# Chunked attention and a maxout layer on one core: where the attention weights of the stacked tiles are transposed

## The chip, the core and the metric

One core of one Trainium2 chip runs the whole program. The metric is the device time of one execution in microseconds; lower is better. Kernels are compared by the median of their runs.

## What is computed

Attention within chunks of 64 positions (8 batches, 8 heads, 576 positions, head size 64), then three products, their maximum, and a last product. All of it is float32:

```
scores = (1 / 8) * q_c @ k_c.T        # q_c, k_c, v_c: chunks of 64 x 64
attn   = exp(scores - max); attn = attn / (sum + 1e-9)
x      = (attn @ v_c), heads side by side      # 4608 tokens x 512
h      = max(x @ w1, x @ w2, x @ w3)           # 4608 x 768
out    = h @ w_out                             # 4608 x 512
```

## The kernel before, in words

The 4608 tokens are 36 tiles of 128 tokens (two chunks, eight heads), and nine groups of four tiles. A group's layer (`moe`) is 18 times 12 products (`hidden`, `pm` in PSUM) and 72 products of the projection (`project`); each product is three matmuls of fp32r (lines 145 to 147), since a float32 value is carried as a high and a low part.

While TensorE works on the layer of group i - 1, the attention of group i is put between its matmuls. TensorE's order is written out by hand: `due` (line 442) gives every step of every tile a time in a count of matmul time, and the loop at the end emits the attention's steps as their times come up. The other engines and the DMA queue (SP) have no order of their own in the source: a scheduler sets it from the data and from the buffers.

Ten tiles are plain. The other 26 are "stacked" (`attention`, line 249), and the change is about these. Their six steps, with their due times in units of that count, are `operands` (-8), `scores(0)` (0), `scores(1)` (2.9), `transpose` (16.5), `values(0)` (25.0) and `values(1)` (28.2). The next tile's `scores(0)` comes 16.3 after this tile's, so tile t's transpose stands right behind `scores(0)` of tile t + 1. Below, t is the tile whose weights are transposed.

- `operands` loads q and k (`r`, 1 MB) and v (`rv`, 512 KB), both with their rows twice, and makes `qs` and `kk`: ScalarE rounds to fp32r, GpSimd subtracts for the low part (`stack`, `split`).
- `scores(c)` runs four matmuls of 256 columns for chunk c into `s` (PSUM, one buffer); ScalarE copies and VectorE adds the two halves into `e`. After c = 1 comes the softmax (VectorE, GpSimd, ScalarE, and at its end GpSimd's multiplication at line 162), and `vs` is made of `rv` (ScalarE line 256, GpSimd line 257).
- `transpose` turns `e` by four TensorE transposes into `tp`; ScalarE and VectorE split it into high and low parts in half of the rows of `aa`, and two DMAs copy each half to the other rows:

```
tp = ps_t.tile([P, 4, P], F32, name="tp")
for g in range(4):
    nc.tensor.transpose(out=tp[:, g, :], in_=..., identity=ident)
...
for c, rows in enumerate(halves_of):
    nc.sync.dma_start(out=aa[halves_of[1 - c], c].bitcast(F32), in_=aa[rows, c].bitcast(F32))
```

- `values(c)` multiplies `vs` by `aa` for chunk c into `x`; `xs` collects the sums, and `xh`, `xl` are the layer's input.

Buffers matter: `aa`, `rv`, `qs`, `kk` and `xs` have one each, `vs` has two (by t modulo 2), `e` has two.

Of the kernel before, what the change touches and what calls it, by code (L numbers as in the profile page):

```python
# [8 lines left out]
F32 = mybir.dt.float32  # L9
F32R = mybir.dt.float32r  # L10
# [4 lines left out]
ALU = mybir.AluOpType  # L15
# [3 lines left out]
B, H, S, D = 8, 8, 576, 64  # L19
P = 128  # L20
# [5 lines left out]
PLAIN = 10  # L26
# [25 lines left out]
def chunk_attn_maxout_kernel(  # L52
# [12 lines left out]
    nc = tc.nc  # L65
# [2 lines left out]

    att = ctx.enter_context(tc.tile_pool(name="att", bufs=1))
    xs_p = ctx.enter_context(tc.tile_pool(name="xs_p", bufs=1))  # L70
    ep = ctx.enter_context(tc.tile_pool(name="ep", bufs=2))
    xp = ctx.enter_context(tc.tile_pool(name="xp", bufs=2))
    hpool = ctx.enter_context(tc.tile_pool(name="hpool", bufs=JT))
    tmp = ctx.enter_context(tc.tile_pool(name="tmp", bufs=2))
# [2 lines left out]
    ps_s = ctx.enter_context(tc.tile_pool(name="ps_s", bufs=1, space=PSUM))  # L77
    ps_t = ctx.enter_context(tc.tile_pool(name="ps_t", bufs=1, space=PSUM))
    ps_x = ctx.enter_context(tc.tile_pool(name="ps_x", bufs=1, space=PSUM))
    ps_m = ctx.enter_context(tc.tile_pool(name="ps_m", bufs=3, space=PSUM))  # L80

    ident = cpool.tile([P, P], F32, name="ident")
# [7 lines left out]
    def split(hi, lo, src, eng=nc.vector):  # L90
        nc.scalar.copy(out=hi, in_=src)  # L91
        eng.tensor_tensor(out=lo, in0=src, in1=hi.bitcast(F32), op=ALU.subtract)  # L92
# [84 lines left out]
    def plain_steps(t, x_of, col):  # L177


        st = {}  # L180

        def load_qk():
            st["r"] = att.tile([P, 1536], F32, name="buf", tag=("raw", "kk", "aa")[t % 3], bufs=1)
            nc.sync.dma_start(out=st["r"], in_=qk[t])

        def load_v():
            st["v"] = att.tile([P, 4, 2, P], F32, name="buf", tag=f"vs{t % 2}", bufs=1)
            nc.sync.dma_start(out=st["v"], in_=vb[t].rearrange("p (g c x) -> p g c x", g=4, c=2))

        def scores():  # L190
            r = st["r"]
            st["s"] = s = ps_s.tile([P, 8, 64], F32, name="s")
            for h in range(8):
                nc.tensor.matmul(out=s[:, h, :], lhsT=r[:, h * P:(h + 1) * P],  # L194
                                 rhs=r[:, 1024 + h * 64:1024 + (h + 1) * 64], start=True, stop=True)

        def maximum():
            st["mx"] = tmp.tile([P, 8], F32, name="mx")
            nc.vector.tensor_reduce(out=st["mx"], in_=st["s"], axis=AX.X, op=ALU.max)

        def less():
            st["e"] = ep.tile([P, 8, 64], F32, name="e")
            nc.vector.tensor_tensor(out=st["e"], in0=st["s"],
                                    in1=st["mx"].unsqueeze(2).broadcast_to([P, 8, 64]), op=ALU.subtract)

        def exp():
            nc.scalar.activation(out=st["e"], in_=st["e"], func=AF.Exp, scale=SCALE)

        def total():
            total, st["guard"], st["invert"], st["norm"] = over_sum(st["e"])  # L210
            total()

        def transpose():
            st["tp"] = tp = ps_t.tile([P, 4, P], F32, name="tp")
            for g in range(4):
                nc.tensor.transpose(out=tp[:, g, :], in_=st["e"][:, 2 * g:2 * g + 2].rearrange("p h k -> p (h k)"),  # L216
                                    identity=ident)

        def transposed():
            st["at"] = xs_p.tile([P, 4, P], F32, name="xs")  # L220
            nc.scalar.copy(out=st["at"], in_=st["tp"])

        def values():
            st["x"] = x = ps_x.tile([P, 4, P], F32, name="x")
            for g in range(4):
                for c in range(2):
                    nc.tensor.matmul(out=x[:, g, c * 64:(c + 1) * 64], lhsT=st["v"][:, g, c, :],  # L227
                                     rhs=st["at"][:, g, c * 64:(c + 1) * 64], start=True, stop=True)

        def high():  # L230
            nc.scalar.copy(out=x_of()[0][:, :, col:col + P], in_=st["x"])

        def low():
            xh, xl = x_of()
            nc.vector.tensor_tensor(out=xl[:, :, col:col + P], in0=st["x"],
                                    in1=xh[:, :, col:col + P].bitcast(F32), op=ALU.subtract)

        return dict(q=load_qk, v=load_v, S=scores, mx=maximum, sub=less, exp=exp, sum=total,
                    eps=lambda: st["guard"](), rec=lambda: st["invert"](), nrm=lambda *eng: st["norm"](*eng),
                    T=transpose, at=transposed, V=values, xh=high, xl=low)  # L240
# [6 lines left out]
    halves_of = [slice(0, 64), slice(64, 128)]  # L247

    def attention(t, x_of, col):

        st = {}

        def stack(hi, src):
            nc.scalar.copy(out=hi, in_=src)  # L256
            nc.gpsimd.tensor_tensor(out=hi[64:], in0=src[64:], in1=hi[64:].bitcast(F32), op=ALU.subtract)  # L257

        def products(pool, name, c, lhs, rhs, out):
            o = pool.tile([P, 4, 2, 2, 64], F32, name=name)  # L260
            for g in range(4):
                nc.tensor.matmul(out=o[:, g].rearrange("p a h x -> p (a h x)"), lhsT=lhs[:, c, g, :],  # L262
                                 rhs=rhs[:, c, g].rearrange("p a x -> p (a x)"), start=True, stop=True)
            for h, rows in enumerate(halves_of):
                nc.scalar.copy(out=out[rows], in_=o[rows, :, 0, h, :])  # L265
            for h, rows in enumerate(halves_of):
                nc.vector.tensor_tensor(out=out[rows], in0=o[rows, :, 1, h, :], in1=out[rows], op=ALU.add)  # L267

        def operands():
            r = att.tile([P, 2, 2, 4, P], F32, name="r", tag="raw", bufs=1)  # L270
            nc.sync.dma_start(out=r, in_=qk2[t - PLAIN])
            rv = att.tile([P, 2, 4, P], F32, name="rv", tag="rv", bufs=1)
            nc.sync.dma_start(out=rv, in_=v2[t - PLAIN])
            qs = att.tile([P, 2, 4, P], F32R, name="qs", tag="qs", bufs=1)
            stack(qs, r[:, 0])
            kk = att.tile([P, 2, 4, 2, P], F32R, name="kk", tag="kk", bufs=1)
            for c in range(2):
                split(kk[:, c, :, 0, :], kk[:, c, :, 1, :], r[:, 1, c], nc.gpsimd)
            st.update(rv=rv, qs=qs, kk=kk)

        def scores(c):
            if c == 0:
                st["e"] = ep.tile([P, 4, 2, 64], F32, name="e")
            products(ps_s, "s", c, st["qs"], st["kk"], st["e"][:, :, c, :])
            if c == 1:
                ef = st["e"].rearrange("p g c k -> p (g c) k")
                softmax(ef)
                vs = st["vs"] = att.tile([P, 2, 4, P], F32R, name="vs", tag=f"vs{t % 2}", bufs=1)
                stack(vs, st["rv"])

        def transpose():
            tp = ps_t.tile([P, 4, P], F32, name="tp")
            for g in range(4):
                nc.tensor.transpose(out=tp[:, g, :], in_=st["e"][:, g].rearrange("p c k -> p (c k)"), identity=ident)  # L294
            st["aa"] = aa = att.tile([P, 2, 4, 2, P], F32R, name="aa", tag="aa", bufs=1)
            for c, rows in enumerate(halves_of):
                nc.scalar.copy(out=aa[rows, c, :, 0, :], in_=tp[rows])
            for c, rows in enumerate(halves_of):
                nc.vector.tensor_tensor(out=aa[rows, c, :, 1, :], in0=tp[rows],
                                        in1=aa[rows, c, :, 0, :].bitcast(F32), op=ALU.subtract)  # L300
            for c, rows in enumerate(halves_of):
                nc.sync.dma_start(out=aa[halves_of[1 - c], c].bitcast(F32), in_=aa[rows, c].bitcast(F32))

        def values(c):
            if c == 0:
                st["xs"] = xs_p.tile([P, 4, P], F32, name="xs")
            products(ps_x, "x", c, st["vs"], st["aa"], st["xs"][:, :, c * 64:(c + 1) * 64])
            if c == 1:
                xh, xl = x_of()
                split(xh[:, :, col:col + P], xl[:, :, col:col + P], st["xs"], nc.gpsimd)  # L310

        return [operands, lambda: scores(0), lambda: scores(1), transpose, lambda: values(0), lambda: values(1)]

    outputs = []
# [138 lines left out]
    with tc.manual_schedule(engines={mybir.EngineType.PE}):  # L453
        for i in range(1, len(GROUPS)):
            g = moe(starts[i], lambda i=i: x_tiles(i))
# [49 lines left out]
```

## Time and profile before

| | |
|---|---|
| median of 3 runs | 713.27 us (713.2 to 714.03) |
| the profiled execution | 713.1 us, span 711.4 us |
| TensorE clock | 2.4 GHz over the whole span (granted clock 1.0) |
| busy share | PE 99%, DVE 56%, ACT 51%, POOL 43% |
| DMA | 90.28 MB moved, 38.5% of the 16 engines' time |

The span is the time from the first to the last instruction in the trace; the execution's own time lies 1.7 us above it. Busy PE is not PE at its peak: matmuls overlap in the pipeline, so the time that one adds is read from the distance between two starts, not from its duration.

### The profile page before, as it was taken

The page shows a single profiled execution, that of the slowest core. Times are in us where ns is not written, and L with a number is a line of the kernel's source. Part 1 is how long each engine was busy: PE and PEld are TensorE (multiplying, and loading weights), DVE is VectorE, ACT ScalarE, POOL GpSimd, SP SyncE. Part 2 cuts the span into 40 slices and gives each one's busy share as a digit, 9 for nine tenths or more (in the row PEclk, how much of TensorE's full clock was granted, in tenths as well). Part 3 has the DMA queues.
Part 4 walks back from the last instruction along what each step waited for, and adds up shares of the span by engine and source line. Part 5 has one row for each costly group of instructions (what it writes and reads, how often), then busy time and mean ns, then how long its engine had stood idle before and what let it go on. Part 6 is the DMA issues. An engine that isn't in the chain of part 4 may idle for free.

```text
span 711.4 us, 9743 instructions
## 1 busy us (share of the span) xinstructions
PE 703.1 (99%) x3545; PEld 592.9 (83%) x3546; DVE 398.9 (56%) x677; ACT 359.8 (51%) x665; POOL 308.9 (43%) x207
## 2 busy tenths in 40 slices
PE   8999999999999999999999999999999999999997
PEld 5997888888888888888888888888888888888886
DVE  7989852456456655676466637664566456521220
ACT  6675551445555555555555555556555655331111
POOL 2443020245656665555665555555566656100000
PEclk9999999999999999999999999999999999999999
DMA  9975640233433354333523363335333541120001
GB/s 365 410 275 185 195 139 31 88 117 114 149 124 119 111 144 131 119 118 84 184 90 118 119 177 119 119 120 171 120 105 107 160 134 33 30 75 15 1 1 59
DMA packets 23215, 90.28 MB, mean 127 GB/s; under 512 B 2944, under 2 KB 2944, under 8 KB 19840
## 3 DMA queue, kind: packets, MB, share of 16 engines
q1 hardware_dynamic: 23168, 89.67, 38.5%
q8 instruction: 28, 0.46, 0.3%
q14 instruction: 19, 0.16, 0.1%
HBM read 66.58 MB, written 9.44 MB: 107 GB/s over the span
## 4 chain that ended last, share of the span: by engine, by line
PE 95%; DMA 2%; DVE 1%; issue 1%; ACT 1%; SPq 0%; POOL 0%; ACTq 0%; DVEq 0%
PE pm L145 27%; PE pm L146 27%; PE pm L147 27%; PE s L262 3%; PE x L262 3%; PE x L227 2%; PE s L194 2%; PE tp L294 2%; DMA buf<-in_w 1%; DMA buf<-in_wout 1%; PE tp L216 1%; ACT ao L117 0%; SPq L108 0%; ACT kk L91 0%; POOL e L162 0%
## 5 line engine op out<-in xcount | busy, mean ns | idle before, releaser
L145 PE MATMUL pm<-xh,wl 128*128 128x512 f32 (+1 forms) x660 | 258.9, 392 | 0.3 <-ACT m L336 0.3
L146 PE MATMUL pm<-xl,wh 128*128 128x512 f32 (+1 forms) x660 | 255.3, 387 | 0.0
L147 PE MATMUL pm<-xh,wh 128*128 128x512 f32 (+1 forms) x660 | 254.9, 386 | 0.0
L147 PEld LDWEIGHTS pm<-xh,wh 128*128 128x128 f32 x660 | 124.1, 188 | 25.8
L145 PEld LDWEIGHTS pm<-xh,wl 128*128 128x128 f32 x660 | 124.4, 188 | 22.7 <-ACT m L336 0.7
L146 PEld LDWEIGHTS pm<-xl,wh 128*128 128x128 f32 x660 | 124.5, 189 | 21.7
L338 DVE TENSOR_TENSOR m<-pm,m 128x512 f32<-128x512 f32 (+1 forms) x110 | 74.9, 681 | 116.1 <-PE pm L147 95.2
L257 POOL TENSOR_TENSOR qs<-r,qs 64x1024 fp32r<-64x1024 f32 x26 | 62.5, 2402 | 148.2 <-ACT qs L256 148.1
L257 POOL TENSOR_TENSOR vs<-rv,vs 64x1024 fp32r<-64x1024 f32 x26 | 62.3, 2397 | 62.5 <-ACT vs L256 62.5
L347 DVE TENSOR_TENSOR hl<-m,hh 128x512 fp32r<-128x512 f32 (+1 forms) x54 | 75.3, 1394 | 17.7 <-ACT hh L344 17.3
L145 PE MATMUL pm<-woh,hl 128*128 128x512 f32 x216 | 85.0, 394 | 0.0
L265 ACT COPY e<-s 64x256 f32<-64x256 f32 x104 | 38.1, 366 | 91.9 <-PE s L262 91.3
L146 PE MATMUL pm<-wol,hh 128*128 128x512 f32 x216 | 84.4, 391 | 0.0
L147 PE MATMUL pm<-woh,hh 128*128 128x512 f32 x216 | 84.2, 390 | 0.0
L267 DVE TENSOR_TENSOR e<-s,e 64x256 f32<-64x256 f32 x104 | 43.8, 421 | 63.6 <-ACT e L265 62.9
L344 ACT CAST hh<-m 128x512 fp32r<-128x512 f32 (+1 forms) x55 | 33.5, 610 | 85.9 <-DVE m L338 85.9
L92 POOL TENSOR_TENSOR kk<-r,kk 128x512 fp32r<-128x512 f32 x52 | 66.7, 1297 | 6.2 <-ACT kk L91 5.7
L267 DVE TENSOR_TENSOR xs<-x,xs 64x256 f32<-64x256 f32 x104 | 43.8, 421 | 30.5 <-ACT xs L265 28.0
L265 ACT COPY xs<-x 64x256 f32<-64x256 f32 x104 | 38.0, 365 | 31.7 <-PE x L262 30.3
L162 POOL TENSOR_TENSOR e<-e,sm 128x512 f32<-128x512 f32 x31 | 32.3, 1043 | 47.0 <-DVE sm L159 43.9
L336 ACT COPY m<-pm 128x512 f32<-128x512 f32 (+1 forms) x55 | 31.8, 579 | 35.6 <-DVE hl L347 22.0
L147 PEld LDWEIGHTS pm<-woh,hh 128*128 128x128 f32 x216 | 40.6, 188 | 8.7
(67 smaller groups left out, 831.4 us busy)
## 6 DMA issues: line engine op xcount, KB each, us to landing
r<-in_qk SPq DMA_DIRECT2D x26, 1024.0 KB, 4.9
rv<-in_v SPq DMA_DIRECT2D x26, 512.0 KB, 3.3
aa<-aa SPq DMA_DIRECT2D x52, 256.0 KB, 3.3
out_x<-ao SPq DMA_DIRECT2D x36, 256.0 KB, 3.6
buf<-in_qk SPq DMA_DIRECT2D x10, 768.0 KB, 7.8
buf<-in_w SPq DMA_DIRECT2D x10, 512.0 KB, 4.5
buf<-in_vb SPq DMA_DIRECT2D x10, 512.0 KB, 6.7
buf<-in_wout SPq DMA_DIRECT2D x6, 512.0 KB, 3.9
```

The costliest lines, as they stand in the source:

```text
L92: eng.tensor_tensor(out=lo, in0=src, in1=hi.bitcast(F32), op=ALU.subtract)
L145: nc.tensor.matmul(out=o, lhsT=al, rhs=bh, start=first, stop=False)
L146: nc.tensor.matmul(out=o, lhsT=ah, rhs=bl, start=False, stop=False)
L147: nc.tensor.matmul(out=o, lhsT=ah, rhs=bh, start=False, stop=last)
L162: eng.tensor_tensor(out=e, in0=e, in1=sm.unsqueeze(2).broadcast_to([P, 8, 64]), op=ALU.mult)
L257: nc.gpsimd.tensor_tensor(out=hi[64:], in0=src[64:], in1=hi[64:].bitcast(F32), op=ALU.subtract)
L262: nc.tensor.matmul(out=o[:, g].rearrange("p a h x -> p (a h x)"), lhsT=lhs[:, c, g, :], rhs=rhs[:, c, g].rearrange("p a x -> p (a x)"), st ...
L265: nc.scalar.copy(out=out[rows], in_=o[rows, :, 0, h, :])
L267: nc.vector.tensor_tensor(out=out[rows], in0=o[rows, :, 1, h, :], in1=out[rows], op=ALU.add)
L338: nc.vector.tensor_tensor(out=banks[j][:, :n], in0=ps[j, w][:, :n], in1=banks[j][:, :n], op=ALU.max)
L344: nc.scalar.copy(out=hh[j][:, lo:hi], in_=banks[j][:, :hi - lo])
L347: eng.tensor_tensor(out=hl[j][:, lo:hi], in0=banks[j][:, :hi - lo], in1=hh[j][:, lo:hi].bitcast(F32), op=ALU.subtract)
```

## The change

Step `transpose` no longer uses TensorE. VectorE transposes `e` in blocks of 32 x 32 (one instruction) into `et`, ScalarE and VectorE split the whole of `et` into `ah` (high and low), and eight DMAs of 128 KB lay it out: a block of 32 partitions of `ah` becomes 64 partitions of `aa` (each source row of 4 KB gives two rows of 2 KB), once for the upper and once for the lower half. `aa` therefore holds its contraction rows in another order, and the host lays out v in the same order. In `values` the moving operand of a matmul is now read in runs of 32 columns (8 runs make 256), where it was one run of 256.

To find room, `ah` shares its only buffer with `rv`, whose load moves from `operands` to `scores(0)`; `e` and `et` have one buffer each (the plain tiles use both in turn, and tiles 8 and 9 use that of `et`). The due times and TensorE's order of the other steps are the same.

```
-    ep = ctx.enter_context(tc.tile_pool(name="ep", bufs=2))
+    ep = ctx.enter_context(tc.tile_pool(name="ep", bufs=1))
...
-            st["e"] = ep.tile([P, 8, 64], F32, name="e")
+            st["e"] = ep.tile([P, 8, 64], F32, name="e", tag="e" if t in (1, 3, 5, 7) else "et")
...
-        def products(pool, name, c, lhs, rhs, out):
+        def products(pool, name, lhs, rhs, out):
...
-                nc.tensor.matmul(out=o[:, g].rearrange("p a h x -> p (a h x)"), lhsT=lhs[:, c, g, :],
-                                 rhs=rhs[:, c, g].rearrange("p a x -> p (a x)"), start=True, stop=True)
+                nc.tensor.matmul(out=o[:, g].rearrange("p a h x -> p (a h x)"), lhsT=lhs[:, g, :], rhs=rhs(g),
+                                 start=True, stop=True)
...
-            rv = att.tile([P, 2, 4, P], F32, name="rv", tag="rv", bufs=1)
-            nc.sync.dma_start(out=rv, in_=v2[t - PLAIN])
...
         def scores(c):
             if c == 0:
                 st["e"] = ep.tile([P, 4, 2, 64], F32, name="e")
+                st["rv"] = att.tile([P, 2, 4, P], F32, name="rv", tag="rv", bufs=1)
+                nc.sync.dma_start(out=st["rv"], in_=v2[t - PLAIN])
...
         def transpose():
-            tp = ps_t.tile([P, 4, P], F32, name="tp")
-            for g in range(4):
-                nc.tensor.transpose(out=tp[:, g, :], in_=st["e"][:, g].rearrange("p c k -> p (c k)"), identity=ident)
-            st["aa"] = aa = att.tile([P, 2, 4, 2, P], F32R, name="aa", tag="aa", bufs=1)
-            for c, rows in enumerate(halves_of):
-                nc.scalar.copy(out=aa[rows, c, :, 0, :], in_=tp[rows])
-            for c, rows in enumerate(halves_of):
-                nc.vector.tensor_tensor(out=aa[rows, c, :, 1, :], in0=tp[rows],
-                                        in1=aa[rows, c, :, 0, :].bitcast(F32), op=ALU.subtract)
-            for c, rows in enumerate(halves_of):
-                nc.sync.dma_start(out=aa[halves_of[1 - c], c].bitcast(F32), in_=aa[rows, c].bitcast(F32))
+            et = ep.tile([P, 2, 8, 32], F32, name="et")
+            nc.vector.transpose(out=et,
+                                in_=st["e"].rearrange("p g c (k x) -> p k (g c) x", k=2))
+            ah = att.tile([P, 2, 2, 8, 32], F32R, name="ah", tag="rv", bufs=1)
+            split(ah[:, :, 0], ah[:, :, 1], et)
+            st["aa"] = aa = att.tile([P, 4, 2, 8, 32], F32R, name="aa", tag="aa", bufs=1)
+            for n in range(4):
+                for rows in halves_of:
+                    nc.sync.dma_start(out=aa[rows, n].bitcast(F32), in_=ah[32 * n:32 * n + 32].bitcast(F32))
...
-            products(ps_x, "x", c, st["vs"], st["aa"], st["xs"][:, :, c * 64:(c + 1) * 64])
+            products(ps_x, "x", st["vs"][:, c], lambda g: st["aa"][:, :, :, 2 * g + c].rearrange("p n a x -> p a n x"),
+                     st["xs"][:, :, c * 64:(c + 1) * 64])
```

How the scheduler's order moves is seen in three places. First ScalarE, around the tile with `e_2993` (tile t + 1); `ah_3007` belongs to tile t. Before:

```order
L256 CAST vs_3035<-rv_2899 128x1024
L336 COPY m_2957<-pm_2933 128x512
L91 CAST xh_2607<-xs_2909 128x4x128
L265 COPY e_2977<-s_2978 64x4x64 x2
L297 CAST aa_2992<-tp_2987 64x4x128 x2
L265 COPY e_2977<-s_3017 64x4x64 x2
```

Of the change:

```order
L256 CAST vs_3055<-rv_2994 128x1024
L338 COPY m_2973<-pm_2949 128x512
L91 CAST xh_2619<-xs_2925 128x4x128
L91 CAST ah_3007<-et_3005 128x2x256
L265 COPY e_2993<-s_2996 64x4x64 x2
L346 CAST hh_3029<-m_2973 128x512
L265 COPY e_2993<-s_3037 64x4x64 x2
```

`vs` of tile t + 1 is made ahead of `ah` of tile t, whose buffer it frees (`rv_2994`), and the cast to `ah` stands ahead of the copies of the next scores.

VectorE at the same place, of the change (`ah` is the subtraction for the low part):

```order
L349 TENSOR_TENSOR hl_2946<-m_2895,hh_2945 128x512
L296 STREAM_TRANSPOSE et_3005<-e_2821 128x512
L267 TENSOR_TENSOR xs_2925<-x_2956,xs_2925 64x4x64 x2
L340 TENSOR_TENSOR m_2973<-pm_2975,m_2973 128x512
L92 TENSOR_TENSOR ah_3007<-et_3005,ah_3007 128x2x256
L267 TENSOR_TENSOR e_2993<-s_2996,e_2993 64x4x64 x2
L340 TENSOR_TENSOR m_2973<-pm_2989,m_2973 128x512
```

Before, the two subtractions for `aa` stood behind the additions to `e` of `scores(0)`; now one stands ahead of them.

The DMA queue, SP, before:

```order
L271 DMA r_3063<-in_qk2 128x2048
L273 DMA rv_3065<-in_v2 128x1024
L302 DMA aa_2992<-aa_2992 64x1024 x2
L271 DMA r_3231<-in_qk2 128x2048
L367 DMA out_x<-ao_3091 128x512
```

Of the change:

```order
L283 DMA rv_2994<-in_v2 128x1024
L271 DMA r_3083<-in_qk2 128x2048
L303 DMA aa_3010<-ah_3007 64x1x512 x8
L283 DMA rv_3162<-in_v2 128x1024
L369 DMA out_x<-ao_3109 128x512
L271 DMA r_3253<-in_qk2 128x2048
```

The load of `rv` now stands behind the eight DMAs that read `ah` from the same buffer, and waits for them; the loads of `r` and the output stand behind it.

## Rows read from the trace of the kernel before

**Rows 1.** The page, part 1: busy time, share of the span, instructions.

```profile
PE 703.1 (99%) x3545; PEld 592.9 (83%) x3546; DVE 398.9 (56%) x677; ACT 359.8 (51%) x665; POOL 308.9 (43%) x207
```

**Rows 2.** The chain that ended last, by source line.

```profile
by line: PE pm L145 27.2%; PE pm L146 27.0%; PE pm L147 27.0%; PE s L262 3.5%; PE x L262 3.5%; PE x L227 2.2%; PE s L194 2.0%; PE tp L294 1.6%; DMA buf<-in_w 1.4%; issue 0.8%; DMA buf<-in_wout 0.6%; PE tp L216 0.6%; ACT ao L117 0.3%; SPq L1
```

**Rows 3.** Timeline of PE: start us, us, engine, line, operation, out<-in, count.

```profile
396.90 0.64 PE L262 MATMUL s<-kk,qs 128*128 128x256 f32 x4
...
397.38 0.60 PE L294 MATMUL tp<-ident,e 128*128 128x128 f32 x4
...
398.28 0.39 PE L147 MATMUL pm<-xh,wh 128*128 128x512 f32 x1
...
400.57 0.64 PE L262 MATMUL s<-kk,qs 128*128 128x256 f32 x4
...
401.04 0.40 PE L145 MATMUL pm<-woh,hl 128*128 128x512 f32 x1
...
401.51 0.39 PE L147 MATMUL pm<-woh,hh 128*128 128x512 f32 x1
```

**Rows 4.** Groups by shape: count, busy us, mean ns, idle before.

```profile
L294 PE MATMUL tp<-ident,e 128*128 128x128 f32 x104 | 15.6, 272 | 0.0
...
L299 DVE TENSOR_TENSOR aa<-tp,aa 64x512 fp32r<-64x512 f32 x52 | 35.8, 689 | 11.0 <-ACT aa L297 10.2
...
L297 ACT CAST aa<-tp 64x512 fp32r<-64x512 f32 x52 | 30.2, 581 | 3.8 <-PE tp L294 2.7
...
L153 DVE TENSOR_REDUCE sm<-e 128x8 f32<-128x512 f32 x36 | 24.6, 684 | 17.6 <-ACT e L170 16.6 <-ACT e L207 0.7
```

**Rows 5.** Timeline, all engines, from 391 us on.

```profile
391.64 0.64 PE L262 MATMUL x<-aa,vs 128*128 128x256 f32 x4
...
393.22 1.05 ACT L256 CAST vs<-rv 128x1024 fp32r<-128x1024 f32 x1
...
394.41 2.40 POOL L257 TENSOR_TENSOR vs<-rv,vs 64x1024 fp32r<-64x1024 f32 x1 [2.17 <-ACT vs L256]
...
396.89 1.28 POOL L92 TENSOR_TENSOR xl<-xs,xh 128x512 fp32r<-128x512 f32 x1
...
398.35 0.85 DVE L267 TENSOR_TENSOR e<-s,e 64x256 f32<-64x256 f32 x2 [1.17 <-ACT e L265]
...
406.51 0.64 PE L262 MATMUL x<-aa,vs 128*128 128x256 f32 x4
```

**Rows 6.** Timeline of GpSimd and VectorE at 384 us.

```profile
384.42 2.40 POOL L257 TENSOR_TENSOR qs<-r,qs 64x1024 fp32r<-64x1024 f32 x1 [5.00 <-ACT qs L256]
...
384.85 2.53 DVE L347 TENSOR_TENSOR hl<-m,hh 128x512 fp32r<-128x512 f32 x1
```

**Rows 7.** Issues and landings of aa (L302), DMA load by window, two loads.

```profile
437.81 1.23 SPq L302 DMA_DIRECT2D aa<-aa  x2
...
L302 SPq DMA_DIRECT2D aa<-aa x52: 461/467/1077, 156.3 to 625.4; - x52
...
DMA to landing us min/median/max: 2.8/3.3/4.2
...
438.80:439.20 0.40, 0.40 (x3) 0.34 (x2) 0.40 (x1) 0.39 (x2) 0.00 (x0) 1.00 0.75 174
...
438.80:441.20 2.40, 2.40 (x12) 1.98 (x11) 2.01 (x5) 2.36 (x5) 0.47 (x1) 1.00 0.85 219
...
455.00:455.40 0.40, 0.40 (x3) 0.31 (x2) 0.39 (x2) 0.38 (x2) 0.00 (x0) 1.00 1.05 389
...
r<-in_qk SPq DMA_DIRECT2D x26, 1024.0 KB, 4.9
...
rv<-in_v SPq DMA_DIRECT2D x26, 512.0 KB, 3.3
```

**Rows 8.** Timeline around the first stacked tile.

```profile
153.02 2.39 POOL L257 TENSOR_TENSOR vs<-rv,vs 64x1024 fp32r<-64x1024 f32 x1 [5.55 <-ACT vs L256]
...
162.54 0.64 PE L262 MATMUL x<-aa,vs 128*128 128x256 f32 x4
```

More of the change, by code (lines that the diff above doesn't have):

```diff
@@ L278, in operands @@
                 split(kk[:, c, :, 0, :], kk[:, c, :, 1, :], r[:, 1, c], nc.gpsimd)
-            st.update(rv=rv, qs=qs, kk=kk)
+            st.update(qs=qs, kk=kk)
         def scores(c):
@@ L283, in scores @@
                 st["e"] = ep.tile([P, 4, 2, 64], F32, name="e")
-            products(ps_s, "s", c, st["qs"], st["kk"], st["e"][:, :, c, :])
+                st["rv"] = att.tile([P, 2, 4, P], F32, name="rv", tag="rv", bufs=1)
+                nc.sync.dma_start(out=st["rv"], in_=v2[t - PLAIN])
+            products(ps_s, "s", st["qs"][:, c], lambda g: st["kk"][:, c, g].rearrange("p a x -> p (a x)"),
+                     st["e"][:, :, c, :])
             if c == 1:
@@ L486 @@
     qk2 = np.repeat(np.concatenate([q2, k2], axis=3), 2, axis=1).reshape(n, P, 2, 2, 4, P)
-    v2 = np.repeat(v[PLAIN:].transpose(0, 3, 1, 2, 4).reshape(n, 1, 64, 2, 4, P), 2, axis=1).reshape(n, P, 2, 4, P)
+    v2 = v[PLAIN:].reshape(n, 2, H, 2, 32, D).transpose(0, 4, 3, 1, 2, 5)
+    v2 = np.repeat(v2.reshape(n, 1, 64, 2, 4, P), 2, axis=1).reshape(n, P, 2, 4, P)
     def bits(a):
```

## The prediction, made before the changed kernel ran

> **What bounds the kernel now.** I began with the busy shares: TensorE is busy 99% of the span, VectorE 56%, ScalarE 51%, GpSimd 43% [rows 1]. The chain of waits confirms it: the three lines of layer matmuls hold 81% of it, the two products of stacked attention 3.5% each, and the transposes that the change removes (`tp`, L294) 1.6%, or 11.4 us of 711.4 [rows 2]. So time that leaves TensorE's order shortens the run, unless TensorE then waits for something it does not wait for now. The granted clock is 1.0 in each stretch read below.
>
> **What leaves TensorE.** The duration of a transpose, 272 ns [rows 4], is not its price, since it overlaps its neighbours. I take the same stretch with and without the four transposes: from the first `s` matmul to the third layer matmul behind it, 398.28 - 396.90 = 1.38 us with them, 401.51 - 400.57 = 0.94 us without [rows 3]. One tile pays 0.44 us, and 26 tiles 26 x 0.44 = 11.4 us, which is the chain's share again. The page "TensorE: Matmul & The Clock Gate" of the Trainium skill, in "Part 4: PE-mode transpose", gives some 275 ns for a transpose in a kernel. As a price per instruction that would be an estimate of 104 x 0.275 = 28.6 us, and a run of some 686 us. The trace agrees with it as a duration and not as a price.
>
> **What replaces it, and what hides it.** Per tile ScalarE loses two casts of 0.58 us and gets one of about 0.6; VectorE loses two subtractions of 0.69 us [rows 4] and gets a transpose and one subtraction of 128 x 512. The transpose is in no row. The nearest, a VectorE instruction that reads 128 x 512 from SBUF alone, takes 0.68 us [rows 4]; I take that, with twice to three times as the far end. Neither engine is full, so what counts is lateness. I follow one tile, on the clock of the old trace.
>
> The normalization of tile t's weights stands ahead of `vs` in GpSimd's queue, which was idle for 2.17 us before `vs` [rows 5]; `et` follows it. That is not what `ah` waits for: it lies in `rv`'s buffer, so it waits until GpSimd has read `rv` of tile t + 1 for `vs`. `vs` in turn needs its older contents to be used up by `values(1)` of tile t - 1, which starts at 391.64. ScalarE's part runs at 393.22, GpSimd's from 394.41 to 396.81 [rows 5]. ScalarE's cast to `ah` then ends near 397.5. VectorE's subtraction comes next, but GpSimd has started `xl` at 396.89 and runs to 398.17 [rows 5]. In this trace VectorE's two-input SBUF instructions do not pass a running GpSimd one: `hl` started at 384.85, inside GpSimd's 384.42 to 386.82, and ended 0.56 us after that, at 387.38 [rows 6]. So the subtraction ends at 398.17 + 0.56 = 398.73, and the DMAs start about 7.1 us after `values(1)` of tile t - 1.
>
> `values(0)` of tile t starts at 406.51 [rows 5], 14.87 us after the same start; without one tile's transposes, 14.43 us. That leaves **7.3 us for eight DMAs**. Their price:
> - Issue to first data: 1.0 us (issued 437.81, the first load is in the window from 438.80) [rows 7].
> - Data: 1.05 MB. Two DMAs from 64 partitions each moved 219 GB/s in the window 438.80 to 441.20 [rows 7], so 4.8 us.
> - Last data to landing: about 0.8 us. The second `aa` DMA, issued 0.76 us behind the first, is through with its data by about 441.1, and a landing comes 3.3 us after its issue at the median [rows 7], here 441.9.
>
> The sum is 6.6 us, 0.7 us to spare. The fast end is set by issuing: 7 x 0.467 us and a landing of 2.8 us [rows 7], 6.1 us. The slow end comes from partitions: a load to all 128 ran at 389 GB/s, one from 64 at 219 [rows 7]; if 32 source partitions halve the rate again, the data takes 9.6 us and the whole 11.4 us, 4.1 us late in each tile. I take 219, because in all eight the other side has 64 partitions as in that row. The Trainium skill speaks to this in "SBUF — State Buffer", "Door 1: The DMA port swizzle": the port follows from certain bits of the partition number, so that 32 neighbouring partitions reach as many ports as 64. By that rule the slow end falls away and the sum stays 6.6 us; no row here shows it.
>
> What waits behind these steps:
> - *VectorE:* the additions to `e` of the next `scores(0)` (0.85 us [rows 5]) now stand behind the subtraction and end at about 399.6 instead of 399.2. `scores(1)` reuses their PSUM buffer at 400.57 - 0.44 = 400.13 [rows 3]: 0.5 us to spare.
> - *GpSimd:* the order sets one `kk` subtraction (1.28 us, as the same shape of `xl`) ahead of the softmax's first, so the normalization ends that much later. The 2.17 us of idle time before `vs` cover it [rows 5]. No cost; if the cover goes, `vs` and with it `ah` are late next.
> - *`e` with one buffer:* the next scores come into it just ahead of 398.35 [rows 5], and the transpose has read it about when `vs` begins on GpSimd, at 394.41. No cost.
> - *SP:* `rv` waits for all eight DMAs, at about 405.4, and lands 3.3 us later [rows 7], some 409. A tile lasts (406.51 - 162.54) / 13 = 18.77 us [rows 5, 8], so ScalarE reads it at 393.22 + 18.77 - 0.44, near 411.6. `r` and outputs stand behind it; `r` lands in 4.9 us [rows 7] and is read only behind the next tile's `scores(1)`. No cost.
> - *Moving operand in runs of 32:* four `x` or `s` matmuls take 0.47 us from start to start [rows 3]. Operands in one run are all that the trace has, so I take no change and twice as the far end: 208 x 0.117 = 24.4 us.
>
> **The first stacked tile** has less room: plain tile 9's values free `vs` late, GpSimd's part ends at 155.41 [rows 8], a cast of 0.6 us, a layer maximum and the subtraction end at about 157.1, and with 6.6 us the DMAs land at 163.7. `values(0)` would start at 162.54 - 0.44 = 162.10 [rows 8]. Cost: 1.6 us, once.
>
> **Sum.** 713.1 - 11.4 + 1.6 = 703.3 us against the profiled execution's own 713.1; the median of the runs is 0.17 higher, so I say 703.5.
>
> **The rivals.**
> 1. *The eight DMAs are late in every tile (slower).* Place: the wait of `values(0)` for `aa`. Price: 26 times what they take over 7.3 us, because each late `values(1)` frees the next `vs` late and nothing catches up. From 7.3 + 9.8/26 = 7.7 us on, the change loses. The first window of the old `aa`, at 174 GB/s with one DMA in flight [rows 7], would give 1.0 + 6.0 + 0.8 = 7.8 us and 703.5 + 26 x 0.5 = 716.5 us; the slow end, 26 x 4.1 more, 810. Against it: two DMAs in flight did better. For it: the room is under 10% of the chain. Late by 0.1 to 0.3 us, it leaves 706 to 711.5.
> 2. *VectorE's transpose is long.* It stands ahead of the additions to `xs`, those ahead of `xh`, and `xh` ahead of `ah` on ScalarE. At 2.1 us `ah` would come about 1.2 us late, and `scores(1)` would wait 0.7 us: 703.5 + 18 = 722.
> 3. *The runs of 32 columns double `values`:* 703.5 + 24 = 728. Nothing for it in the trace but that it has no such matmul.
> 4. *The gain is hidden:* TensorE waits about as long as it saves, at one of the two points with half a microsecond to spare. 713, no change.
> 5. *The transposes' price is their duration:* 104 x 0.272 = 28.3 us [rows 4], so 687. Rows 3 speak against it.
>
> **How the numbers follow.** No steady wait, 701 to 706 us: 0.57. Rival 1 in part (706 to 711.5): 0.10; rival 1 in full: 0.17. Rival 2: 0.04. Rival 3: 0.04. Rival 4: 0.06. Rival 5: 0.02. A difference below 0.2%, or 1.4 us, is what a measurement of this kernel can't tell from none. Faster is 0.57 + 0.10 + 0.02 = 0.69, the same 0.06, slower 0.25. The range runs from 701 (no cost at the first tile, and the DMAs at their fast end) to 720: it leaves out rivals 2, 3 and 5, some of the low edge, and the far part of rival 1, together 0.2. The likeliest case's own range is 701 to 706.
>
> **What would show it.** Right: `tp` of L294 is gone from TensorE and from the chain; `x` (L262) has no idle time ahead of it but once near 162 us; the eight DMAs land 6 to 7 us after the first is issued; the distance between the same steps of two tiles falls by 0.44 us; the subtraction for `ah` ends some 0.6 us after GpSimd's `xl`. Wrong: a wait of `x` for `aa` in each tile (rival 1), a wait of `s` for VectorE (rivals 2 and 4), four `x` matmuls over 0.47 us apart (rival 3). A VectorE transpose well over 0.7 us, or an issue on SP over 0.6 us, would undo the sum first.

## The result, and the profile after

The changed kernel takes 716.36 us (median of 6 runs, 714.12 to 717.25); the kernel before takes 713.62 us beside it (6 runs, 713.2 to 714.1). The ratio is 1.0035, with an interval of 1.002 to 1.0051: slower, by a little. The forecast was 703.5 us and faster. The profiled execution took 716.68 us, span 714.9.

The page, part 1, and the chain by line, of the changed kernel:

```profile
PE 699.0 (98%) x3442; PEld 580.8 (81%) x3442; DVE 380.9 (53%) x677; ACT 351.2 (49%) x639; POOL 302.1 (42%) x207
...
PE pm L145 24%; PE pm L147 23%; PE pm L146 23%; SPq L303 4%; PE x L262 4%; PE s L262 3%; PE x L227 2%; PE s L194 2%; DMA aa<-ah 2%; DMA out_x<-ao 1%; POOL vs L257 1%; DVE ah L92 1%; PE tp L216 1%; ACT vs L256 1%; DMA xh<-in_w 1%
```

Against [rows 1] every engine does less, and the chain has lost `tp` of L294 [rows 2]. In its place stand the eight DMAs: their issuing on SP (L303) with 4% and their landing with 2%, some 43 us of 715. The chain runs through the issues of all eight DMAs in six of the 26 tiles (from 157, 178, 309, 385, 516 and 572 us), and stays on TensorE in most others.

TensorE's timeline over one tile (start us, us, engine, line, operation, count):

```profile
396.50 0.64 PE L262 MATMUL x<-aa,vs 128*128 128x256 f32 x4
...
401.79 0.64 PE L262 MATMUL s<-kk,qs 128*128 128x256 f32 x4
...
405.01 0.64 PE L262 MATMUL s<-kk,qs 128*128 128x256 f32 x4
...
410.95 0.73 PE L262 MATMUL x<-aa,vs 128*128 128x256 f32 x4
...
414.94 0.64 PE L262 MATMUL x<-aa,vs 128*128 128x256 f32 x4
```

From `scores(0)` to `scores(1)` are 405.01 - 401.79 = 3.22 us, where it was 400.57 - 396.90 = 3.67 [rows 3]: the transposes' price is 0.45 us a tile. `values(1)`, with the operand in runs of 32 columns, takes 0.64 us as in [rows 5]. `values(0)` takes 0.73 us here: the load of its first weights has waited 0.2 us for the last DMA.

What is lost again shows best in distances between the same steps, not in the list of waits. The waits of TensorE, longest first (us in all, times, longest):

```profile
PE x L262 <- DMA aa<-ah: 5.6, 5, 2.5
PE pm L424 <- DVE hl L426: 1.5, 1, 1.5
PE x L262 <- issue: 1.4, 3, 0.7
```

They name 7 us for `x`. The distances from `scores(1)` of a tile to `values(0)` of the tile before it, 5.94 us each in the trace before (406.51 - 400.57 [rows 3, 5]), are longer by 2.65 us at the first stacked tile and by 7.7 us together in the 24 tiles behind it, 11 to 34.

The distances that start at the two `x` of a tile are longer too, by 2.7 us in all without the first stacked tile. About half of that is no wait. TensorE's `values(0)` before (its `values(1)` starts at 391.64 [rows 5]), then both of tile 14 of the change, where the DMAs came in time:

```profile
387.74 0.64 PE L262 MATMUL x<-aa,vs 128*128 128x256 f32 x4
...
242.10 0.64 PE L262 MATMUL x<-aa,vs 128*128 128x256 f32 x4
...
246.02 0.64 PE L262 MATMUL x<-aa,vs 128*128 128x256 f32 x4
```

The step from `values(0)` to `values(1)` is 3.92 us instead of 3.90, and 3.92 to 3.94 in tiles 13, 14, 30, 31 and 35, whose DMAs came in time; the step behind `values(1)` is 0.03 longer in every tile. So `x`, with the layer matmuls behind it, costs some 0.05 us a tile in itself. Why is open. The rest, 1.4 us, is starting up again behind waits. With these, the two profiled executions differ by:

| | us |
|---|---|
| transposes, 26 x 0.45 | -11.7 |
| first stacked tile: wait 2.65, then matmuls at the lower clock 1.7 | +4.4 |
| waits of `x` in tiles 11 to 34 | +7.7 |
| starting up again behind them | +1.4 |
| the two `x` in themselves, 26 x 0.05 | +1.3 |
| the first `scores(0)` of a stacked tile starts 0.47 us later | +0.5 |
| sum (the spans differ by 714.9 - 711.4 = 3.5) | +3.6 |

The last term varies from one execution to the next: in the profiled executions of the experiments below it is 0.05 to 2.3 us.

The groups of the steps that are new, by shape (count, busy us, mean ns, idle before):

```profile
L92 DVE TENSOR_TENSOR ah<-et,ah 128x512 fp32r<-128x512 f32 x26 | 31.0, 1191 | 22.0 <-ACT ah L91 21.2
L296 DVE STREAM_TRANSPOSE et<-e 128x512 f32<-128x512 f32 x26 | 18.3, 702 | 7.4 <-POOL e L162 7.3
L91 ACT CAST ah<-et 128x512 fp32r<-128x512 f32 x26 | 16.2, 622 | 28.1 <-POOL vs L257 21.2 <-DMA out_x<-ao 4.1 <-DVE et L296 1.7
```

The engines' parts are as forecast: 0.70 us for the transpose (0.68 was taken), 0.62 for the cast. ScalarE's cast waits for `vs` on GpSimd, as the sum said. The eight DMAs are not as forecast (issue ns, least, median and most; then issue to landing, us):

```profile
L303 SPq DMA_DIRECT2D aa<-ah x208: 537/601/1985, 157.5 to 627.1; - x104
...
DMA to landing us min/median/max: 2.6/2.7/4.4
```

The chain that starts them, on all engines:

```profile
396.48 0.62 ACT L346 CAST hh<-m 128x512 fp32r<-128x512 f32 x1 [1.76 <-DVE m L340]
...
397.18 0.75 ACT L265 COPY xs<-x 64x256 f32<-64x256 f32 x2
397.95 1.05 ACT L256 CAST vs<-rv 128x1024 fp32r<-128x1024 f32 x1
...
399.13 2.40 POOL L257 TENSOR_TENSOR vs<-rv,vs 64x1024 fp32r<-64x1024 f32 x1 [1.19 <-ACT vs L256]
...
401.57 0.62 ACT L91 CAST ah<-et 128x512 fp32r<-128x512 f32 x1 [1.05 <-POOL vs L257]
401.62 1.29 POOL L92 TENSOR_TENSOR xl<-xs,xh 128x512 fp32r<-128x512 f32 x1
...
402.22 1.23 DVE L92 TENSOR_TENSOR ah<-et,ah 128x512 fp32r<-128x512 f32 x1 [0.15 <-ACT ah L91]
...
403.54 5.06 SPq L303 DMA_DIRECT2D aa<-ah  x8
```

The first DMA is issued at 403.54, 7.04 us after `values(1)` at 396.50 (forecast 7.1), and VectorE's subtraction ends at 403.45, 0.54 us after GpSimd's `xl` (forecast 0.56). In tiles 11 to 34 the start lies 7.02 to 7.05 us after `values(1)` of the tile before. But one DMA is issued every 0.64 us, so eight take 5.06 us, and `x` starts 2.35 us behind the end of the last issue: 7.41 us, where 7.3 was the room and 6.6 the sum. The window of its data (busy us of PE, PEld, DVE, ACT, POOL; granted clock; DMA share; GB/s):

```profile
404.75:410.20 5.45, 5.45 (x27) 4.57 (x26) 2.69 (x5) 3.44 (x6) 2.35 (x1) 1.00 0.79 191
```

Over tiles 11 to 34 the time from the first issue to `x` is 7.40 to 8.75 us, 7.74 at the mean.

Where no issue is stretched, it is 7.4 to 7.8 us. The long ones come from single stretched issues. SP's timeline in the tile at 309 us:

```profile
311.78 1.59 SPq L303 DMA_DIRECT2D aa<-ah  x1
```

The DMA queues of the stretch 309.2 to 315.4 (packets, MB, share of 16 engines), and last that of 403.5 to 408.7, a tile without such an issue:

```profile
q1 hardware_dynamic: 463, 0.77, 53.6%
q8 instruction: 1, 0.02, 1.5%
...
q1 hardware_dynamic: 459, 0.76, 62.8%
```

An issue of 1.59 us stands where a packet of instruction code (16 KB, queue q8) is loaded. The same holds at 253, 384 and 440 us, with issues of 1.28 to 1.35 us, and the stretches at 403 and 421 us have neither. Over the whole trace each of the eight issues of 1.28 us or more has such a load beside it, and no such load falls among the issues without one; the trace before has five such pairs, with issues of 0.82 to 1.08 us, hidden by some 2 us between the last landing and `x`. In eight of the 24 tiles the issues take over 5.2 us together, and these eight make 6.1 of the 7.7 us of waits. That the load causes the stretch is a reading of this coincidence; no run took the loads away.

TensorE's timeline at the first stacked tile:

```profile
165.24 0.72 PE L262 MATMUL x<-aa,vs 128*128 128x256 f32 x4 [2.49 <-DMA aa<-ah]
...
167.35 0.63 PE L146 MATMUL pm<-xl,wh 128*128 128x512 f32 x1
```

Two windows there (columns as above):

```profile
166.00:168.00 2.00, 2.00 (x6) 1.54 (x5) 1.12 (x4) 0.73 (x2) 0.00 (x0) 0.50 0.98 324
168.00:169.00 1.00, 1.00 (x3) 0.77 (x3) 0.00 (x0) 0.00 (x0) 0.89 (x1) 0.50 1.07 451
```

TensorE stands idle for 2.49 us, and from about 166 to 169 us its granted clock is 0.50, the lower of its levels, 1.2 GHz. The next `x` comes 5.58 us later instead of 3.90: that delay of 2.65 us cost 4.4 in all.

### The profile page after: what moved, and what is told of

Its sections match the earlier page's. It is cut to its first block, busy times and chain, and to the rows that moved or that the text cites. A ratio compares the mean times of both kernels' runs of the same rounds, so it can differ in the third digit from the quotient of the medians.

```text
span 714.9 us, 9929 instructions
## 1 busy us (share of the span) xinstructions
PE 699.0 (98%) x3442; PEld 580.8 (81%) x3442; DVE 380.9 (53%) x677; ACT 351.2 (49%) x639; POOL 302.1 (42%) x207
## 4 chain that ended last, share of the span: by engine, by line
PE 82%; SPq 4%; DMA 4%; ACT 3%; DVE 3%; POOL 2%; issue 2%; POOLq 0%; ACTq 0%; DVEq 0%
PE pm L145 24%; PE pm L147 23%; PE pm L146 23%; SPq L303 4%; PE x L262 4%; PE s L262 3%; PE x L227 2%; PE s L194 2%; DMA aa<-ah 2%; DMA out_x<-ao 1%; POOL vs L257 1%; DVE ah L92 1%; PE tp L216 1%; ACT vs L256 1%; DMA xh<-in_w 1%
## 5 line engine op out<-in xcount | busy, mean ns | idle before, releaser
L349 DVE TENSOR_TENSOR hl<-m,hh 128x512 fp32r<-128x512 f32 (+1 forms) x54 | 49.3, 912 | 25.1 <-ACT hh L346 24.8
L146 PEld LDWEIGHTS pm<-wol,hh 128*128 128x128 f32 x216 | 40.6, 188 | 7.8 <-POOL wol L140 0.2
L145 PEld LDWEIGHTS pm<-woh,hl 128*128 128x128 f32 x216 | 40.6, 188 | 7.7
```

The costliest lines, as they stand in the source:

```text
L145: nc.tensor.matmul(out=o, lhsT=al, rhs=bh, start=first, stop=False)
L146: nc.tensor.matmul(out=o, lhsT=ah, rhs=bl, start=False, stop=False)
L349: eng.tensor_tensor(out=hl[j][:, lo:hi], in0=banks[j][:, :hi - lo], in1=hh[j][:, lo:hi].bitcast(F32), op=ALU.subtract)
```

## The experiments

Theory A: `x` waits because the eight DMAs start too late for what they take; within it, A1 says that issuing them on one queue sets what they take, A2 that the bytes do. The first runs vary the start, the queue, the number and the room.

**The load of `rv` behind (e1).**

```
         def scores(c):
             if c == 0:
                 st["e"] = ep.tile([P, 4, 2, 64], F32, name="e")
+            if c == 1:
                 st["rv"] = att.tile([P, 2, 4, P], F32, name="rv", tag="rv", bufs=1)
                 nc.sync.dma_start(out=st["rv"], in_=v2[t - PLAIN])
```

> Edit: the load of rv moves from scores(0) to scores(1), so that ah of tile t takes the shared buffer before rv of tile t + 1 and no longer waits for vs of tile t + 1. Theory A (the eight DMAs start too late for the 7.4 to 8.4 us that they need; nothing else is wrong): they start 2 to 3 us earlier after values(1) of the tile before (now 7.0 us after it), x has no steady idle time, the first stacked tile neither, and the time is 713.1 - 11.4 + 0 to 2 = 702 to 704 us. Rival B (x costs more in itself, by its operand in runs of 32 or by waiting for eight DMAs): x still loses some 0.4 us per tile, and the time stays over 711. Rival C (rv now lands too late and takes the place of the old wait): x or vs waits for rv, over 713.

Measured: 747.69 us, ratio 1.048 (1.0448 to 1.0511). Rival C, at a place that I had not seen. One tile on all engines:

```profile
343.01 0.33 SPq L284 DMA_DIRECT2D rv<-in_v  x1
...
346.25 1.05 ACT L256 CAST vs<-rv 128x1024 fp32r<-128x1024 f32 x1 [4.96 <-DMA rv<-in_v]
347.33 0.75 ACT L265 COPY xs<-x 64x256 f32<-64x256 f32 x2
...
348.16 0.86 DVE L267 TENSOR_TENSOR xs<-x,xs 64x256 f32<-64x256 f32 x2 [7.38 <-ACT xs L265]
...
349.16 0.36 PE L262 MATMUL x<-aa,vs 128*128 128x256 f32 x1 [1.77 <-DVE xs L267]
```

`values(0)` had started at 343.31. The scheduler had put the cast to `vs` ahead of the copies of `x` on ScalarE; there it waits 4.96 us for `rv`, and the copies, VectorE's additions and `values(1)` (one buffer of `x`) wait behind it. The first stacked tile, though, lost nothing, and the distance to `values(0)` grew by only 1.8 us in all tiles together: the DMAs' start was mended (5.0 to 6.8 us behind `values(1)` instead of 7.0), and a new wait took its place.

**Two queues (e2).**

```
-                    nc.sync.dma_start(out=aa[rows, n].bitcast(F32), in_=ah[32 * n:32 * n + 32].bitcast(F32))
+                    (nc.sync if rows.start else nc.scalar).dma_start(out=aa[rows, n].bitcast(F32), in_=ah[32 * n:32 * n + 32].bitcast(F32))
```

> Edit: of the eight DMAs the four to the upper rows stay on SP's queue and the four to the lower rows go to ScalarE's. Theory A1 (one queue's issues, 0.63 us each, set the pace): both queues are through after 2.5 us and the last DMA lands about 5.5 us after the first is issued instead of 7.2; steady waits of x go, and the time is 703 to 707 us, the first stacked tile's wait of some 4 us shorter by 1 to 2. Rival A2 (the data sets the pace, at the 200 GB/s that the windows show): 1.05 MB take 5.1 us as before, the last landing stays near 7 us, and the time stays at 714 to 718.

Measured: 815.43 us, ratio 1.1427 (1.1409 to 1.1445). One tile's queues and ScalarE:

```profile
359.99 3.60 ACTq L303 DMA_DIRECT2D aa<-ah  x4
360.04 3.56 SPq L303 DMA_DIRECT2D aa<-ah  x4
363.63 0.74 ACT L265 COPY e<-s 64x256 f32<-64x256 f32 x2 [4.64 <-issue]
```

The window of its DMAs, columns as above:

```profile
361.10:366.40 5.30, 5.30 (x21) 4.30 (x20) 1.53 (x3) 2.73 (x5) 0.81 (x1) 0.82 0.85 197
```

Each queue now takes 0.9 us for an issue (SP's median is 900 ns, ScalarE's 854), the data takes 5.3 us at 197 GB/s, and `x` starts 7.56 us behind the first issue. Over tiles 11 to 34 the eight issues are through 1.5 us sooner than in the changed kernel, but the last DMA lands only 0.2 us sooner (7.1 us behind the first issue instead of 7.3, medians): A1 alone is not the whole, a second limit near 5.3 us lies right behind the issues. Whether the bytes set it or two queues at once, no run tells apart. The 100 us come mostly from elsewhere: ScalarE's copies of `e` wait 4.64 us behind its own issues, the next scores wait for them, and the DMAs start up to 11.8 us behind `values(1)` instead of 7.0. Of TensorE's waits:

```profile
PE s L262 <- DVE e L267: 46.1, 23, 2.5
PE x L262 <- DMA aa<-ah: 29.6, 19, 2.5
```

The Trainium skill, page "DMA: Bandwidth & Descriptors", section "Issuing engines are not separate DMA queues", says that issuing on several engines saves only the sequencer's time to start a DMA, which is usually small beside the DMA. The first half agrees: 1.5 us of issuing were saved, and hardly anything else. The second half is less clear in the changed kernel, where one issue is 0.60 us of the 2.7 to its landing, but eight in a row are 5.06 of 7.41 us.

**Sixteen DMAs (e3).**

```
-                    nc.sync.dma_start(out=aa[rows, n].bitcast(F32), in_=ah[32 * n:32 * n + 32].bitcast(F32))
+                    for i in range(2):
+                        nc.sync.dma_start(out=aa[rows.start + 32 * i:rows.start + 32 * i + 32, n].bitcast(F32),
+                                          in_=ah[32 * n + 16 * i:32 * n + 16 * i + 16].bitcast(F32))
```

> Edit: sixteen DMAs of 64 KB (16 source partitions each) instead of eight of 128 KB, same bytes, same rows. Theory A1 with a price per DMA (0.6 us each): 16 issues take 10 us, x waits some 5 us more in each tile, and the time is above 830 us. Price per row of a DMA (64 rows take 0.6 us, 32 take 0.3): issues take 5 to 6 us together, and the time stays within 716 to 725. Rival A2 (data): issues take what they take, and the time stays near 716.

Measured: 880.12 us, one run. The group of the issues:

```profile
L304 SPq DMA_DIRECT2D aa<-ah x416: 567/591/1696, 157.0 to 794.9; - x139
```

One tile's sixteen on SP's timeline:

```profile
309.68 10.12 SPq L304 DMA_DIRECT2D aa<-ah  x16
```

An issue costs 0.59 us with half the rows and half the bytes. The price of an issue is per DMA. `x` comes 4.5 to 6.0 us late in each of tiles 11 to 34, and each time 1.4 to 3.0 us more are lost between the two `x`, at a mean granted clock of 0.55 to 0.77.

**Room by the due times (e4, e7).**

```
e4:
-            at = ... (-8.0, 0.0, 2.9, 16.5, 25.0, 28.2)]
+            at = ... (-8.0, 0.0, 2.9, 16.5, 25.0, 27.5)]
e7:
+            at = ... (-8.0, 0.0, 2.9, 16.5, 25.7, 28.2)]
```

A product in the expectations is three matmuls, some 0.68 us; a group's layer has 18 times 4 products and 24 of the projection, and the 12 and 72 named with the kernel before are matmuls.

> Edit: values(1) is due at 27.5 instead of 28.2, one product of 0.68 us nearer to values(0), so that the eight DMAs have 0.68 us more room in each tile and nothing else changes. Theory A: each steady wait shrinks by up to 0.68 us. The waits of x from tile 11 on add up to 7.7 us now; cut by 0.68 each they leave 1.5, so the time falls by 6 to 8 us to 708 to 711; the first stacked tile keeps its wait. Rival B (x costs more in itself): no change, 715 to 718.

> Edit: the changed kernel with values(0) due at 25.7 instead of 25.0 alone; where e4 moved values(1), whose copies then waited on ScalarE behind the cast to hh, this leaves the start of the DMAs as it is (7.0 us after values(1) of the tile before) and gives them 0.68 us more. Theory A: of the steady waits (7.7 us) 1.5 us are left, of the first stacked tile's 4.4 us about 3.7: 713.1 - 11.4 + 1.5 + 3.7 + 1 = 707 to 709 us. If it stays over 712, the room is not what x lacks.

Measured: 712.84 us for e4 (ratio 0.9978, 0.9966 to 0.999) and 711.38 us for e7 (0.9965, 0.9952 to 0.9978). Both win against the kernel before, less than said: the waits of tiles 11 to 34 are 4.0 and 3.8 us instead of 7.7, where 1.5 had been expected. ScalarE in e4, and TensorE's `values(1)` there:

```profile
300.54 0.62 ACT L346 CAST hh<-m 128x512 fp32r<-128x512 f32 x1 [1.75 <-DVE m L340]
301.18 0.74 ACT L265 COPY xs<-x 64x256 f32<-64x256 f32 x2
301.95 1.05 ACT L256 CAST vs<-rv 128x1024 fp32r<-128x1024 f32 x1
...
299.89 0.64 PE L262 MATMUL x<-aa,vs 128*128 128x256 f32 x4
```

`values(1)` is through at 300.53, but the copies of its result stand behind the cast to `hh` until 301.18; that hangs on VectorE's maximum, and that on the sums for the copies of `values(0)`. So the start has two paths of almost the same length, 7.0 us from `values(1)` and 11.0 us from `values(0)`. In e4 and e7 it lies 7.5 to 7.7 us behind `values(1)` in most tiles, and 10.8 to 11.0 behind `values(0)`, as before. Only the first tile of each group (12, 16 and so on), where no cast to `hh` stands there, gained its 0.68 us.

**Number against bytes (e8, e9).**

```
e8:
-            for n in range(4):
-                for rows in halves_of:
-                    nc.sync.dma_start(out=aa[rows, n].bitcast(F32), in_=ah[32 * n:32 * n + 32].bitcast(F32))
+            for rows in halves_of:
+                nc.sync.dma_start(out=aa[rows].bitcast(F32), in_=ah.bitcast(F32))
e9:
-                    nc.sync.dma_start(out=aa[rows, n].bitcast(F32), in_=ah[32 * n:32 * n + 32].bitcast(F32))
+                    nc.sync.dma_start(out=aa[rows, n].bitcast(F32), in_=ah[32 * n:32 * n + 32, :, 0].bitcast(F32))
```

> Edit: two DMAs of 512 KB, each of all of ah to one half of aa, instead of eight of 128 KB; the same bytes, but the rows come in another order, so the values are not the reference's. Theory A1 (the number of DMAs on one queue sets the pace): issues take 1.2 us, the second lands 4.5 to 6.5 us after the first is issued, the steady waits go, and the time is 703 to 707 us (the first stacked tile may still lose 1 to 3). Rival A2 (the bytes set the pace at 200 GB/s): the second lands 7 us after, and the time stays at 712 to 718.

> Edit: eight DMAs again, but of 64 KB: only the high part is moved, and values uses it for both parts, so half the bytes with the same number of DMAs, rows and matmuls (the low part is left out of the result). Theory A1 (in the changed kernel the pace is that of issuing, 0.63 us a DMA whatever it moves): the eight issues still take 5.06 us, x starts 7.2 to 7.4 us after the first, the waits stay, 713 to 717 us. Rival A2 (the bytes set the pace): issues shorten, x no longer waits in the steady tiles, 703 to 707 us.

Measured: e8 833.7 us, e9 706.19 us, one run each. For e8 the window of one tile's data (the landings, 8.6 us at the median, tell the same):

```profile
230.30:238.10 7.80, 6.40 (x31) 5.02 (x29) 3.43 (x6) 4.03 (x7) 4.58 (x3) 1.00 1.05 134
```

For e9 the issues and landings:

```profile
L303 SPq DMA_DIRECT2D aa<-ah x208: 537/598/1938, 158.4 to 616.2; - x104
...
DMA to landing us min/median/max: 2.1/2.1/3.9
```

e8 went as neither theory said: with two issues, 1.2 us together, the same bytes keep the 16 engines full (share 1.05) at 134 GB/s, and `x` starts 11.1 us behind the first issue. Here the issues are no limit, and the data moves slower than eight DMAs moved it. Why is open. In e9 the eight issues take 5.03 to 5.06 us with half the bytes in each tile without a stretched issue, as A1 says; only the landing is 0.6 us shorter, so that the last one comes 6.6 us behind the first issue (median of tiles 11 to 34) where it was 7.3. Its time proves less than it seems: the DMAs no longer wait for VectorE's subtraction, so they start 5.7 us behind `values(1)` instead of 7.0, and with 8.7 us of room no tile from 11 on waits. It is the start that this run shows.

**The order mended (e5, e6, e10).** The load as in e1, and a step of its own for `vs` that stands behind the exponential on ScalarE (not shown: `softmax` hands back its exponential as `st["exp"]`; in e10 `copied[0]` is the latest copy in `products`):

```
-                vs = st["vs"] = att.tile([P, 2, 4, P], F32R, name="vs", tag=f"vs{t % 2}", bufs=1)
-                stack(vs, st["rv"])
...
+        def stacked():
+            vs = st["vs"] = att.tile([P, 2, 4, P], F32R, name="vs", tag=f"vs{t % 2}", bufs=1)
+            with tc.issue_after(st["exp"]):
+                stack(vs, st["rv"])
...
-            at = ... (-8.0, 0.0, 2.9, 16.5, 25.0, 28.2)]
+            at = ... (-8.0, 0.0, 2.9, 10.0, 16.5, 25.0, 28.2)]
e6, besides:
+            at = ... (-8.0, 0.0, 2.9, 10.0, 16.5, 25.7, 28.2)]
e10, besides e5:
+            with tc.issue_after(st["exp"]), tc.issue_after(copied[0]):
```

> Edit: as in e1 the load of rv stands in scores(1), so that ah takes the shared buffer first; and the step that makes vs is pinned on ScalarE behind the exponential, which e1 let stand ahead of the copies of x. Theory A (x waits only because the eight DMAs start too late): they start 9.4 to 9.8 us after values(0) of the tile before instead of 11.0, so 1.2 to 1.6 us of room are won, more than the longest steady wait (1.2 us); the first stacked tile, whose ah no longer waits for vs of the next tile, loses nothing either. 713.1 - 11.4 + 0 to 2 = 702 to 704 us. Rival C again (vs waits for rv on ScalarE and holds up the copies of x): idle time of x for VectorE, over 710 us.

> Edit: e5, and values(0) due at 25.7 instead of 25.0, one product of 0.68 us later. If anything of the wait for the DMAs is left in e5, this takes it away: 701.5 to 703 us, and no more than 1 us under e5. If e5 waits for something else than the DMAs, it gives nothing or loses.

> Edit: e5, and the step that makes vs is pinned on ScalarE behind the copies of the latest x as well. In e5 the last stacked tile has no exponential late enough to hold it back, and x there waits 1.7 us for VectorE. Expected: that wait goes, all else stays: 1.5 to 1.8 us under e5, so 705 to 707 us by its median of 707.7, ratio to the kernel before near 0.989. If nothing is won, that wait was not what the end hung on.

Measured: e5 707.69 us (ratio 0.9915, 0.9899 to 0.9931), e6 707.44 us (0.9922, 0.9909 to 0.9935), e10 705.19 us (0.9875, 0.9854 to 0.9896), the last against a kernel before at 714.21. e10 is the fastest, faster than both kernels. Its chain in one tile, whose `values(1)` starts at 222.73:

```profile
222.63 2.40 POOL L259 TENSOR_TENSOR vs<-rv,vs 64x1024 fp32r<-64x1024 f32 x1 [0.89 <-ACT vs L258]
...
225.11 1.37 POOL L162 TENSOR_TENSOR e<-e,sm 128x512 f32<-128x512 f32 x1
...
227.91 1.01 DVE L92 TENSOR_TENSOR ah<-et,ah 128x512 fp32r<-128x512 f32 x1 [0.69 <-ACT ah L91]
...
229.01 0.54 SPq L307 DMA_DIRECT2D aa<-ah  x1
```

GpSimd starts `vs` 2.7 us earlier against `values(1)` than in the changed kernel, and the DMAs start 6.28 us behind that step (over the tiles 5.5 to 6.8), with 8.17 us of room. No wait of `x` for a DMA is left in any tile, and `x` waits 0.6 us for GpSimd once; in e5 they come to 0.3 us together, so more room (e6) gives nothing. The one other wait of e5, 1.7 us at the last tile but one, is gone in e10. Theory A is what the three kernels show. Rival B, 0.4 us a tile in `x` itself, is out; what is left of it are the 0.05 us a tile of above, which e5, e9 and e10 have too (3.93 us from `values(0)` to `values(1)` in tiles without a wait). With that, e5's profiled execution (705.93 us) is placed against 702 to 704 us: 1.8 us at the last tile but one, 1.0 where the first stacked tile begins later, 0.3 for the DMAs, and some 1.4 in `x` itself. e5's other runs go up to 709.62, and no trace tells why.

## Why the prediction was wrong

- *What leaves TensorE:* right. 0.44 us a tile was said, 0.45 measured; rival 5 (0.272 us per transpose) is out.
- *The engines' parts and the start of the DMAs:* right in the path and the size, 7.1 us said and 7.03 measured, with the 0.56 us behind GpSimd's `xl` measured as 0.54. What it did not see is the second path of the same length, from `values(0)` over the cast to `hh`.
- *The room of 7.3 us:* right (7.4 us in the trace after).
- **The price of the eight DMAs is the step that failed.** The sum took 1.0 us to the first data, 4.8 us of data at 219 GB/s and 0.8 us to landing, 6.6 us, with issuing as the fast end at 0.467 us a DMA. In the tile at 403.54 the same three terms are 1.2, 5.45 (191 GB/s in the window 404.75 to 410.20) and 0.75 us to the start of `x`, 7.4 in all: the data term was the one mis-sized, and the 0.7 us to spare are gone. The forecast took rate and issue price from DMAs between 64 and 64 partitions of 256 KB each [rows 7]. The rate itself was not far off, 191 GB/s where the row had 219. The port rule of the Trainium skill that the prediction cited ("SBUF — State Buffer", "Door 1: The DMA port swizzle"), by which 32 neighbouring partitions reach as many ports as 64, agrees with that: the rate did not halve. The new ones cost 0.60 us an issue and 0.04 us between two, so 5.06 us for eight; e3 and e9 show that this price goes neither by bytes nor by rows. Why it is 0.60 here and 0.467 there is open. Nor is it shown to be the only limit: with the issues done in 3.6 us (e2) the data still took 5.3 us. And single issues stretched to 1.3 to 2.0 us in seven of tiles 11 to 34 take the mean to 7.74 us; in the 16 tiles with issues under 5.2 us it is 7.5. [rows 7] had such an issue in their maximum, 1077 ns, and the sum went by the median alone. That over 0.6 us an issue would undo the sum was said at the end of the prediction, and not carried into its range of the likeliest case.
- *No steady wait:* wrong by 9.1 us, 7.7 of waits and 1.4 of starting up behind them. Rival 1 named the place. The mean lateness is 0.3 us a tile, which by its price gives 711 us, at the border of its two bands; the other 5 us up to 716 come from terms that it did not hold (the first stacked tile, starting up, `x` in itself). That its example of 7.8 us and a rate of 174 GB/s gives 716.5 us is luck. Eight tiles in which the issues take over 5.2 us, the tiles right behind two of them, and 0.1 to 0.4 us in the first tile of most groups make the 7.7 us; as each late `values(1)` starts the next chain late, nothing is caught up.
- *The first stacked tile:* 1.6 us said, 4.4 measured. The DMAs took 7.75 us, 1.15 more than the sum (they started 0.4 us later than said, but so did the whole tile, by 0.47); and the fall of the clock behind the wait, 1.7 us, was in no term.
- *Rivals 2 and 3* are out: a transpose of 0.70 us, no wait of `s` behind the transposes, and `values(1)` in 0.64 us. The term that the forecast put at nothing, `x` with its operand in runs of 32, measured 0.05 us a tile and 1.3 us in all, where rival 3 had 24.

## What to carry to other kernels

Price a DMA by its count on the queue as well as by its bytes, from the row with the most similar shape, and give the step that rests on it a range that holds the next worse row, and the row's maximum where there is little to spare: here 7.4 us instead of 6.6 used up the room, and a few long issues then went straight into the time. Issues through 1.5 us sooner brought the landing only 0.2 us forward (e2). Where a shared buffer orders two tiles, look at who takes it first, and before moving a load to mend that, look at what stands behind its reader in that engine's queue: e1 lost 33 us against the kernel before by one cast, the same edit with the cast pinned won 6 (e5), and with a second pin 9 (e10). Add up a change from distances between the same steps, since starting up behind a wait and a lower clock stand in no list of waits.

## What was not expected of the hardware

- A DMA issue on SP took 0.59 to 0.60 us for 64 KB and 128 KB alike, where 0.467 us was the median before [rows 7] and the load of `rv` takes 0.33 us (343.01 above).
- Two queues at once did not issue faster together than 0.45 us a DMA (eight in 3.6 us), and the last DMA landed 0.2 us sooner.
- Two DMAs of 512 KB moved their bytes at 134 GB/s with all engines busy, eight of 128 KB at 191 GB/s with a share of 0.79.
- A single wait of 2.49 us on TensorE was followed by some 3 us at a granted clock of 0.50. The length of the wait alone does not decide it: in e2 `x` of the same tile came as late (2.6 us), and the granted clock behind it stayed at 1.0, with 4.00 us to the next `x`.
- A 16 KB load of instruction code beside the issues went with one issue of 1.28 to 1.99 us instead of 0.60, in all eight cases of the changed kernel.
